# Moving filler matmuls into the idle stretch of a kernel's first transposes, and regrouping two pairs of weight blocks

## The chip, the cores and the metric

The kernel runs on one core of a Trainium2 chip. The metric is the device time of one execution in microseconds. Every timed comparison ran on one chip, kernel and kernel before in turns; the four jobs of experiments ran on four chips, so only ratios are compared between jobs. A ratio is the mean time of one kernel's runs over the mean of the other's of the same rounds, so it isn't quite the ratio of the medians that are quoted beside it. A ratio counts as faster or slower from 2% on, which is 5.9 us here.

## The reference

A retention layer (attention with a decay in place of a softmax) feeds a dense layer with gelu:

```python
scores = q @ k^T / sqrt(64)                  # batch 8, heads 8, sequence 576, head size 64
ret    = scores * Dmat                       # gamma_h ** (i - j) where i >= j, else 0
x      = (ret @ v) -> [4608, 512]
h      = x @ w_in                            # [4608, 2048]
out    = (h * sigmoid(1.702 * h)) @ w_out    # [4608, 512]
```

Inputs and output are float32. The kernel computes in bf16, with sums in float32.

## The kernel before

The 4608 rows are cut into 36 units of 128. A lead-in takes units 0 to 3 one by one as their loads arrive: transpose K and Q on TensorE, scores, masked products, and the running state. Then come the up-projections (`up`, `up_group`) of these four units and the down-projections (`down`). From unit 8 on, the transposes are done by DMA. GpSimd issues all loads in one queue, and the first DMA transpose is made to wait for the V load of unit 13 (into buffer `vn1`).

TensorE starts slowly. In the trace of before, K's first transposes (128 columns each, from 4.31 us) start 106 ns apart and Q's (from 5.58 us) 56 ns apart. The text calls the first pace half clock and says that the clock is open at the second; the granted clock doesn't show the difference (1.00 in every stretch of before from 0 us on). So the kernel gives TensorE fillers, matmuls on zeros whose results nobody reads. That their activity opens the clock is its author's assumption.

```python
def warm(n, b='A', w=512):                   # n fillers of w columns
    for i in range(n):
        op("pe", lambda e: e.matmul(bank[b][:, 0:w], gT[1][:, 0, 0:P], gT[1][:, 0, 0:w], ...))

def lead_in():
    load_kq0(0); load_kq0(1)                 # K and Q of unit 0, in float32, on SP's queue
    ...                                      # loads of units 0 to 11, w_in and w_out, on GpSimd's
    warm_quads(NQUAD)                        # 50 fillers of 64x64
    warm(42, "A", 64)
    ...
    cast_kq0(0, "dve")                       # K, then Q, to bf16 on VectorE
    cast_kq0(1, "dve")
    transpose_pe(0, 0, "E")                  # K's transposes into bank E
    transpose_copy(0, 0, "E", "dve")
    warm(1)
    transpose_pe(0, 1, "B")                  # Q's transposes
    transpose_copy(0, 1, "B", "dve")
    ...
    up_group(0, 6, 2, 0, 2, "B")             # chunk, first w_in block, blocks, first unit, end, bank
    up_group(0, 6, 2, 2, 3, "A")
    up_group(0, 0, 4, 3, 4, "C")
    up_group(0, 4, 4, 3, 4, "B")
    ...
    for f in range(8, NF):
        up(0, f)                             # 512 columns: the "full-width up-projections"
```

Engines are kept in order by semaphores that the program works out from reads and writes. Each TensorE matmul comes with a weight load of its own (the page of before has 3,651 weight loads and, with 31 records missing, 3,620 matmuls), so one matmul is two instructions.

## Time and profile before

| | before |
|---|---|
| median of the first three runs | 295.36 us (295.32 to 296.08) |
| span of the profiled run | 293.8 us |
| TensorE busy | 97% |
| unit 0: start of K's and of Q's transposes | 4.31, 5.58 us |
| full-width up-projections begin | 24.3 us |
| unit 5: Q lands, its transposes start | 40.18, 40.31 us |
| unit 9: DMA transpose lands, scores start | 68.19, 68.24 us |

The page of the profile gives busy shares and the chain that ended last. The timeline gives, for each group of instructions, start, length, engine, line and operation, and in brackets the idle time of the engine before it with what ended it. "issue" in a bracket means that the profile shows nothing that the engine waited for. Landing times of loads and times of single DMA packets come from the trace's DMA records. In six traces (before, after and the four of job 1) 31 matmul records are missing, so a group's count can be one short there, and such a gap can look like a stall of 0.16 us. The first full-width up-projection is one of them: its start is taken as 0.22 us ahead of the second's. The lines themselves are in the prediction.

### The profile page before, as it was taken

Reading aid. Unit: us, or ns where it says so; the run is one execution under the profiler, and the core shown is the slowest. Engines: PE = TensorE matmul, PEld = TensorE weight load, DVE = VectorE, ACT = ScalarE, POOL = GpSimd, SP = SyncE. Lnnn points to the kernel's source line nnn. Section 1 sums busy time; section 2 is a strip of 40 time slices with the busy share of each in tenths; the row PEclk is TensorE's granted clock in tenths of the full one; section 3 lists DMA queues with packets and bytes.
Section 4 is the critical chain, followed back from the end, with each engine's and each line's share of the span. In section 5 each row is a group of like instructions: output and inputs, shape, how many; then the busy total and the mean of one; then the engine's idle time right before and its main releaser. Section 6 shows DMA issues by size and latency. Waiting matters only on the chain.

```text
span 293.8 us, 8029 instructions
## 1 busy us (share of the span) xinstructions
PE 284.2 (97%) x3620; PEld 140.7 (48%) x3651; DVE 99.0 (34%) x202; ACT 134.0 (46%) x235; POOL 110.4 (38%) x141
## 2 busy tenths in 40 slices
PE   6899999999999999999999999999999999999996
PEld 5575446775533553345434543454344434443344
DVE  6750056614650643044503460237014700410000
ACT  7556235661366135622563247424642365216611
POOL 9999889000970670291039202910180000000000
PEclk9999999999999999999999999999999999999999
DMA  9999999998999999399379935991691050111022
GB/s 173 171 205 206 206 233 249 233 126 190 146 239 123 128 207 228 77 168 192 110 123 148 195 96 121 171 191 72 146 139 68 22 134 2 38 71 38 0 64 79
DMA packets 116786, 40.63 MB, mean 138 GB/s; under 512 B 104080, under 2 KB 109968, under 8 KB 116752
## 3 DMA queue, kind: packets, MB, share of 16 engines
q0 software_dynamic: 79712, 22.82, 67.7%
q1 hardware_dynamic: 36896, 17.24, 23.7%
q8 instruction: 28, 0.46, 0.6%
q10 hardware_dynamic: 144, 0.07, 0.1%
q14 instruction: 6, 0.05, 0.1%
HBM read 36.70 MB, written 9.44 MB: 157 GB/s over the span
## 4 chain that ended last, share of the span: by engine, by line
PE 75%; POOL 16%; DMA 5%; issue 2%; SPq 1%; DVE 0%; POOLq 0%
PE psB L582 18%; PE psA L582 18%; PE psA L556 17%; PE psB L556 16%; POOL kqn L226 8%; DMA vn<-in_v_dram 4%; POOL vn L239 4%; POOL w_in_sb L261 3%; PE psX L481 1%; POOL w_out_sb L268 1%; DMA kqT<-kqn 1%; SPq L391 1%; PE psC L497 1%; PE psX L519 1%; PE psK L426 1%
## 5 line engine op out<-in xcount | busy, mean ns | idle before, releaser
L226 POOL DMA_DIRECT2D kqn<-in_k_dram x39 | 35.1, 911 | 107.7 <-DMA kqT<-kqn 105.3
L582 PE MATMUL psA<-w_out_sb,gT 128*128 128x512 bf16 (+1 forms) x287 | 65.9, 370 | 2.4 <-issue 2.2
L582 PE MATMUL psB<-w_out_sb,gT 128*128 128x512 bf16 (+1 forms) x285 | 64.7, 376 | 0.5 <-issue 0.5
L556 PE MATMUL psB<-xT,w_in_sb 128*128 128x512 bf16 x233 | 61.4, 379 | 0.4
L556 PE MATMUL psA<-xT,w_in_sb 128*128 128x512 bf16 x239 | 61.4, 379 | 0.1
L544 DVE TENSOR_TENSOR xT<-psX,gq 128x512 bf16<-128x512 f32 x16 | 11.1, 691 | 112.7 <-PE psX L519 112.7
L450 ACT ACTIVATE kv<-stm 128x1024 bf16<-128x1024 f32 (+1 forms) x18 | 15.6, 866 | 68.8 <-DVE stm L441 68.8
L582 PEld LDWEIGHTS psB<-w_out_sb,gT 128*128 128x128 bf16 x288 | 27.8, 98 | 32.5 <-ACT gT L561 0.3
L561 ACT ACTIVATE gT<-psB 128x512 bf16<-128x512 f32 x60 | 35.8, 597 | 15.9 <-PE psB L556 15.7
L561 ACT ACTIVATE gT<-psA 128x512 bf16<-128x512 f32 x60 | 35.8, 597 | 15.7 <-PE psA L556 15.7
L582 PEld LDWEIGHTS psA<-w_out_sb,gT 128*128 128x128 bf16 x304 | 27.2, 98 | 31.7 <-ACT gT L561 2.5
L239 POOL DMA_DIRECT2D vn<-in_v_dram x40 | 37.1, 942 | 0.1
L556 PEld LDWEIGHTS psA<-xT,w_in_sb 128*128 128x128 bf16 x240 | 19.1, 97 | 32.6 <-ACT gT L561 16.6
L556 PEld LDWEIGHTS psB<-xT,w_in_sb 128*128 128x128 bf16 x240 | 18.8, 97 | 33.2 <-ACT gT L561 16.3
L226 POOL DMA_DIRECT2D kqn<-in_q_dram x37 | 33.4, 916 | 0.3 <-issue 0.3
L345 DVE TENSOR_TENSOR vp<-vn,vfac 128x512 bf16<-128x512 f32 x36 | 23.4, 684 | 29.0 <-DMA vn<-in_v_dram 29.0
L592 ACT ACTIVATE osb<-psB 128x512 f32<-128x512 f32 (+1 forms) x18 | 10.6, 591 | 22.4 <-PE psB L582 22.3
L592 ACT ACTIVATE osb<-psA 128x512 f32<-128x512 f32 x18 | 10.5, 584 | 15.3 <-PE psA L582 15.3
L506 DVE TENSOR_TENSOR pm<-psC,mask 128x512 bf16<-128x512 f32 (+1 forms) x20 | 12.6, 628 | 9.0 <-PE psD L497 9.0
L506 DVE TENSOR_TENSOR pm<-psD,mask 128x512 bf16<-128x512 f32 (+1 forms) x20 | 12.5, 626 | 0.0
L570 PE MATMUL psB<-xT,w_in_sb 128*128 128x256 bf16 (+1 forms) x104 | 12.5, 265 | 0.0
L441 DVE TENSOR_TENSOR stm<-psE,stm 128x256 f32<-128x256 f32 x28 | 11.9, 424 | 1.2
(86 smaller groups left out, 254.8 us busy)
## 6 DMA issues: line engine op xcount, KB each, us to landing
vn<-in_v_dram POOLq DMA_DIRECT2D x32, 256.0 KB, 5.5
out_dram<-osb SPq DMA_DIRECT2D x31, 256.0 KB, 2.3
kqn<-in_k_dram POOLq DMA_DIRECT2D x31, 128.0 KB, 5.3
kqn<-in_q_dram POOLq DMA_DIRECT2D x31, 128.0 KB, 5.6
w_out_sb<-in_moe_w_out_dram POOLq DMA_DIRECT2D x4, 512.0 KB, 13.7
w_in_sb<-in_moe_w_in_dram POOLq DMA_DIRECT2D x8, 128.0 KB, 5.0
w_in_sb<-in_moe_w_in_dram POOLq DMA_DIRECT2D x4, 256.0 KB, 7.6
vn<-in_v_dram POOLq DMA_DIRECT2D x8, 128.0 KB, 3.4
```

Source lines behind the costliest of these rows:

```text
L226: e.dma_start(kqn[sl][p0 : p0 + n, which, :, :], src[b, :, s0 : s0 + n, :].rearrange("h p d -> p h d"),)
L239: e.dma_start(vn[sl][p0 : p0 + n, :, :], v[b, :, s0 : s0 + n, :].rearrange("h p d -> p h d"))
L345: op(eng, lambda e: e.tensor_tensor(vp[u % NVP].ap(), vn[sl].ap(), vfac[:, ty, :, None].to_broadcast([P, H, DH]), ALU.mult), reads=[f"vn{s ...
L441: op("dve", lambda e: e.tensor_tensor(dst, src, prev, ALU.add), reads=[KB[a], f"stm{(i - 1) % 8}"], writes=[f"stm{i % 8}"])
L450: op("act", lambda e: e.activation(kv[:, i0 % NKV : i0 % NKV + n, :, :], stm[:, i0 % 8 : i0 % 8 + n, :, :], AF.Copy), reads=[f"stm{(i0 + i ...
L506: op("dve", lambda e: e.tensor_tensor(pm[(u0 // 2) % 2][hh][:, c0:c1].rearrange("p (a i) -> p a i", i=64), ps32(SB[hh])[:, c0:c1].rearrang ...
L544: op("dve", lambda e: e.tensor_tensor(xT[ch % 2][:, slice(hh, 4, 2), P * jj : P * jj + 2 * P].rearrange("p g (u t) -> p u g t", u=2), ps32 ...
L556: op("pe", lambda e, a=a: e.matmul(bank[b][:, n0:n1], w_in_sb[:, a, P * f : P * f + P], xT[c % 2][:, a, n0:n1], start=(a == 0), stop=(a == ...
L561: op("act", lambda e: e.activation(gT[c % 2][:, f, n0:n1], bank[b][:, n0:n1], AF.Gelu_apprx_sigmoid), reads=[b], writes=[f"g{c % 2}_{f}_{j ...
L570: op("pe", lambda e, a=a, f=f, i=i: e.matmul(bank[b][:, n * i : n * i + n], w_in_sb[:, a, P * f : P * f + P], xT[c % 2][:, a, P * lo : P * ...
L582: op("pe", lambda e, f=f: e.matmul(bank[b][:, 0 : n1 - n0], gT[c % 2][:, f, P * r : P * r + P], w_out_sb[:, f, n0:n1], start=(f == 0), sto ...
L592: op("act", lambda e: e.activation(dst, src, AF.Copy), reads=[b], writes=[f"osb{i}_{n0}"])
```

## The change

It moves fillers. More of them now stand ahead of the first transposes and in the idle time between K's and Q's, meant to keep TensorE active until its clock opens, and fewer in unit 1. It also regroups the last products of the lead-in: the w_in pair 6, 7 is taken for units 2 and 3 in one group.

```diff
-NQUAD = 50
+NQUAD = 54
-            warm(42, "A", 64)
+            warm(44, "A", 64)
             cast_kq0(0, "dve")
-            cast_kq0(1, "dve")
             transpose_pe(0, 0, "E")
             transpose_copy(0, 0, "E", "dve")
-            warm(1)
+            cast_kq0(1, "dve")
+            warm(4)
             transpose_pe(0, 1, "B")
 ...
-            gq_next(1)
+            warm(1, "A", 256)
             state_half(0, 0)
             transpose_pe(1, 0, "E")
             transpose_copy(1, 0, "E", "act")
-            warm(2)
 ...
             block1(0)
-            warm(1)
+            warm(1, "A", 256)
             scores(1)
 ...
-            warm(2)
+            gq_next(1)
+            warm(1)
             state_half(1, 0)
 ...
             up_group(0, 6, 2, 0, 2, "B")
-            up_group(0, 6, 2, 2, 3, "A")
             up_group(0, 0, 4, 3, 4, "C")
-            up_group(0, 4, 4, 3, 4, "B")
+            up_group(0, 4, 2, 3, 4, "A")
+            up_group(0, 6, 2, 2, 4, "B")
```

In matmuls, the first two parts add 7 and the regrouping takes 8 away. Behind it the stream is one matmul, two instructions, shorter than before.

## The prediction

> **What bounds the kernel now.** I read the page first. TensorE is busy for nearly the whole span, so the natural reading is that any microsecond saved on it is a microsecond of the total.
>
> ```profile
> span 293.8 us, 8029 instructions
> ...
> PE 284.2 (97%) x3620; PEld 140.7 (48%) x3651; DVE 99.0 (34%) x202; ACT 134.0 (46%) x235; POOL 110.4 (38%) x141
> ...
> DMA  9999999998999999399379935991691050111022
> ...
> PE 75%; POOL 16%; DMA 5%; issue 2%; SPq 1%; DVE 0%; POOLq 0%
> ```
>
> The last line contradicts that reading. It is the chain that ended last, and only 75% of it is TensorE; 16% is GpSimd issuing DMAs and 5% is DMA. The DMA row is full for its first quarter (40 slices of 7.35 us, so to about 65 us). So I asked for the same chain in order of time, to find where it leaves the DMAs.
>
> ```profile
> 48.55 1.71 POOL kqn L226 x2
> 50.26 12.58 DMA vn<-in_v_dram
> 62.93 2.42 SPq L391
> 65.47 2.73 DMA kqT<-kqn
> 68.84 0.81 PE psA L582 x3
> ```
>
> Columns: start, length, what. Until 50.26 us the chain is GpSimd issuing loads one after another from 1.42 us. The last of them (V of unit 13, issued at 50.26) lands 12.58 us later: it stood behind a queue of others. The first DMA transposes (L391) are told to wait for it. TensorE takes the chain over only at 68.24 us, with the scores of unit 9, when the second of those transposes has landed (65.47 + 2.73 = 68.20). The time before 68 us is therefore set by the load queue, and the 225.6 us from there to 293.8 by TensorE.
>
> How far is TensorE ahead of the loads? For that I read its timeline (start, length, instruction; the idle time before and who ended it in brackets).
>
> ```profile
> 4.31 0.61 PE L361 MATMUL psE<-ident,kqn 128*128 128x128 bf16 x4
> 5.58 0.40 PE L361 MATMUL psB<-ident,kqn 128*128 128x128 bf16 x4 [0.67 <-DVE kqn L257]
> ...
> 8.51 0.41 PE L356 MATMUL psB<-ident,kqn 128*64 128x128 bf16 x8 [0.34 <-DMA kqn<-in_q_dram]
> ...
> 39.67 0.40 PE L361 MATMUL psE<-ident,kqn 128*128 128x128 bf16 x4
> 40.31 0.38 PE L361 MATMUL psD<-ident,kqn 128*128 128x128 bf16 x4 [0.24 <-DMA kqn<-in_q_dram]
> ```
>
> The first two are the transposes of unit 0's K and Q: the 0.67 us between them is the idle stretch that the change wants to fill. The third waits for unit 1's Q, whose DMA lands at 8.46. The last two are unit 5's K and Q. The Q transposes could have started 0.06 after the last K one (39.67 + 0.40 - 0.22 = 39.85), at 39.91; they start at 40.31 on a landing at 40.18. So TensorE comes there 0.40 us too early. At the K transposes just ahead it also waits: VectorE's scale of unit 4's V starts at 38.59 on a landing (38.57), its copy out of bank E ends at 39.61, and only then may unit 5's K be written at 39.67, while the matmuls before it (four from 38.60, 0.216 each) leave TensorE free at 39.46. That is another 0.21. And at unit 9's scores:
>
> ```profile
> 68.23 0.10 PEld L497 LDWEIGHTS psC<-kqT 64*64 64x64 bf16 x1 [0.26 <-DMA kqT<-kqn]
> ```
>
> Unit 8's scores start at 67.77 and take about 0.15, so unit 9's could start near 67.93: 0.31 us of waiting.
>
> [...] the four transposes at 4.31 start 106 ns apart, those at 5.58 56 ns apart. So the clock opens between 4.7 and 5.6 us, inside the stretch being filled; this is what the fillers are for. [...]
>
> **The change part by part.**
>
> *Ahead of the first transposes*: 4 more small fillers (50 of them start within 0.66 us: 0.013 each, 0.05) and 2 more of 64 columns (53 ns each at the half clock, 0.11). TensorE reaches the K transposes at 4.31 + 0.16 = 4.47; the cast they need ended at 4.26, so all 0.16 counts here.
>
> *The copy of K's transposes goes ahead of Q's cast on VectorE.* Before, Q's cast starts at 5.10, the copy at 5.44. After: transposes end at 4.47 + 0.61 = 5.08, the copy starts at 5.13, and the cast follows 0.34 later (the spacing of these two before) at 5.47. It ends at 5.90 instead of 5.53. Q's transposes move from 5.58 to 5.95.
>
> *Four fillers of 512 columns instead of one* lie in that stretch: from 4.87, 4 x 0.216 = 0.86 at full clock, to 5.73, hidden before 5.95. If the clock opens as late as 5.6, two of them take 0.43 and they end at 6.16: 0.2 on the path.
>
> Then Q's copy ends at 6.82, the scores of unit 0 start at 6.88 to 7.09 instead of 6.50, V's scale at 6.74 instead of 6.36, the first state update at 7.47 instead of 7.10, unit 1's K transposes at 7.71 instead of 7.34. The lead-in loses about 0.4 to 0.6 here. But unit 1's Q lands at 8.46, and TensorE, free at 7.94 to 8.15, still waits. At 8.51 both kernels stand level.
>
> *Unit 1's fillers*: one of 512 shortened to 256 ahead of the scores saves 0.11; one of the two after them dropped saves 0.22. That is 0.32, but the limit after it is VectorE: both mask products of unit 1, which start where V's landing (9.23) lets them, end at 11.27, so unit 1's value matmuls can start at 11.32 instead of 11.48: 0.16 left. The factor table (0.68 on VectorE) moves to a VectorE gap of 0.83 before 12.10; no cost. At 14.62 the second w_in pair, landed at 14.64, takes 0.06 of it; unit 3's Q, landed at 16.67, holds its transposes at 16.71 in both; what is left comes through VectorE's output of unit 2 at 17.3: about 0.1.
>
> *Regrouping*: 8 x 128 and 16 x 128 columns become 8 x 128 and 8 x 256. Eight pairs at 2 x 56 ns become eight at 109 ns: 0.02 saved. The same number of gelu instructions, in another order; the weight pairs have long landed (20.07).
>
> Sum: TensorE enters the full-width up-projections (24.34) about 0.1 us earlier, between -0.1 and +0.2. At unit 5 it meets V4 and Q5, whose landings this does not move. The wait of 0.40 becomes 0.50. From 40.31 on nothing differs. The net is 0.0.
>
> **The rivals.** (a) *TensorE-bound throughout, the saving reaches the end.* For it: 97% busy. Against: the three waits on landings above. It would give at most 0.1 to 0.3: 295.1. (b) *The lead-in gets slower and it shows*: the cast is later, the fillers may run at half clock. To show, the loss would have to survive 8.51, then exceed 0.21 + 0.40 = 0.6 at unit 5 and another 0.31 at unit 9, some 0.9 us; I see at most 0.6 before 8.51. [...] (c) *The clock opens more surely*: one of the three runs before took 296.08, the others 295.32 and 295.36; if that one was a late clock, the new fillers would remove it, which the median hardly shows. (d) *The load queue itself moves*: [...] I estimate up to 0.3 either way, because the queue is backed up from about 12 us (issue to landing grows from 4.4 to over 10 us by 17).
>
> **Range and chances.** The centre is the median before, since the net is nil. The runs before spread by 0.76 us (the profiled one took 295.64), and that noise comes with the same landings in the new kernel, more upward than downward. A gain much under 295.0 would need the queue to be faster, a loss over 296 one of the accidents in (b). 2% is 5.9 us, ten times any term here. So 295.4 us, from 294.9 to 295.9, faster by over 2% with 0.01, within 2% with 0.98, slower with 0.01.
>
> **What would show it right or wrong.** Right: Q's transposes of unit 0 near 6.0 instead of 5.58; unit 1's Q transposes still at about 8.5 on the DMA; the full-width up-projections within 0.2 us of 24.3; a wait on Q5 near 40.3 at least as long as before; unit 9's scores near 68.2 on the DMA transpose; an equal length from there to the end. Wrong: unit 5's and unit 9's waits gone or a landing moved by over 0.3 us; start-to-start times of 107 ns for 128 columns after 6.5 us; or a difference that arises after 70 us.

The sum came to about 0.1 us earlier at 24.3 us and to 0.0 at the end, hence 295.4 us. The term from (b) stood outside the sum, as a possible total of about 296 us, and is what "the accidents in (b)" refers to. In the DMA passage stood also that the 12.58 us of V from issue to landing compare with 5.5 us, the page's median for the V loads of 256 KB, and that nothing in the change touches what the DMA engines carry.

## The result, and the profile after

Beside before on one chip, the changed kernel took 294.97 us (294.80 to 295.13, four runs) against 295.48 us (295.32 to 296.08, four runs), a ratio of 0.9979 with a 95% interval of 0.9962 to 0.9996. The time as such is just inside the predicted range. The ratio isn't: applied to the 295.36 us of the prediction it is 294.74 us, below the 294.9 that was set as the low end. The prediction had expected no difference.

The page of the changed kernel, the lines that answer to those of before:

```profile
span 293.0 us, 8028 instructions
...
PE 284.6 (97%) x3619; PEld 141.4 (48%) x3650; DVE 99.3 (34%) x202; ACT 133.9 (46%) x235; POOL 110.3 (38%) x141
...
PE 96%; issue 2%; DVE 1%
```

The span is 0.8 us shorter, and the chain that ended last no longer passes through the loads: it is TensorE throughout. So in this execution the loads never held TensorE by much. The timeline of TensorE shows how it got there:

```profile
4.42 0.61 PE L361 MATMUL psE<-ident,kqn 128*128 128x128 bf16 x4
5.25 1.35 PE L674 MATMUL psA<-gT 128*128 128x512 bf16 x3 [0.22 <-issue]
6.43 0.39 PE L361 MATMUL psB<-ident,kqn 128*128 128x128 bf16 x4
...
8.51 0.30 PE L356 MATMUL psB<-ident,kqn 128*64 128x128 bf16 x4
...
39.22 0.39 PE L361 MATMUL psE<-ident,kqn 128*128 128x128 bf16 x4
39.60 0.38 PE L361 MATMUL psD<-ident,kqn 128*128 128x128 bf16 x4
```

The fillers (second line, the first of the four isn't recorded) start 0.43 us apart, at half clock (the two from 6.66 us on are 0.216 apart), and end about 6.4. Q's transposes come at 6.43 instead of 5.58, and unit 1's Q again at 8.51: the lead-in pays for the fillers and gets it back, as predicted. The full-width up-projections then begin at 24.09 instead of 24.34 (the first recorded ones at 24.31 and 24.55). But unit 5's Q, which TensorE had waited for until 40.31, is now there at 39.60, since it landed at 39.47 instead of 40.18. And unit 9's scores start at 67.30 instead of 68.24.

The loads as a whole weren't faster: the V of unit 13 landed at 62.97, against 62.84 before. What was faster is the first DMA transpose. Here is SP's issue of it in the timeline of before, then in that of after:

```profile
62.93 2.42 SPq L391 DMA_TRANSPOSE kqT<-kqn  x1
```

```profile
63.06 1.37 SPq L391 DMA_TRANSPOSE kqT<-kqn  x1
```

SP needed 1.05 us less to issue it, and the second transpose, the one that unit 9 needs, landed 4.29 us after V instead of 5.35 us.

Something was also lost, far from all that was changed. The timeline at 220 us of before, then of after:

```profile
219.77 2.55 PE L582 MATMUL psA<-w_out_sb,gT 128*128 128x512 bf16 x10
```

```profile
219.77 0.81 PE L582 MATMUL psA<-w_out_sb,gT 128*128 128x512 bf16 x3
220.89 0.59 PE L582 MATMUL psA<-w_out_sb,gT 128*128 128x512 bf16 x2 [0.32 <-issue]
```

TensorE stands for 0.32 us in the midst of identical down-projections, and nothing in the profile holds it. In this profile of before, that stall was 0.07 us.

### The profile page after: what moved, and what is told of

It is laid out like the page before. It is cut to its first block, busy times and chain, and to the rows that moved or that the text cites. A ratio compares the mean times of both kernels' runs of the same rounds, so it can differ in the third digit from the quotient of the medians.

```text
span 293.0 us, 8028 instructions
## 1 busy us (share of the span) xinstructions
PE 284.6 (97%) x3619; PEld 141.4 (48%) x3650; DVE 99.3 (34%) x202; ACT 133.9 (46%) x235; POOL 110.3 (38%) x141
## 4 chain that ended last, share of the span: by engine, by line
PE 96%; issue 2%; DVE 1%
PE psA L582 21%; PE psB L582 21%; PE psA L556 18%; PE psB L556 18%; PE psB L570 4%; PE psA L570 3%; PE psX L481 2%; PE psA L674 2%; PE psC L497 1%; PE psY L519 1%; PE psX L519 1%; PE psK L426 1%; PE psE L361 1%; PE psE L426 1%; PE psD L497 1%
## 5 line engine op out<-in xcount | busy, mean ns | idle before, releaser
L570 PE MATMUL psB<-xT,w_in_sb 128*128 128x256 bf16 x96 | 12.5, 273 | 0.0
```

What stands on the lines that cost most here:

```text
L570: op("pe", lambda e, a=a, f=f, i=i: e.matmul(bank[b][:, n * i : n * i + n], w_in_sb[:, a, P * f : P * f + P], xT[c % 2][:, a, P * lo : P * ...
```

## The experiments

Fifteen runs in four jobs. Before's median in the later jobs was 295.73, 295.97, 296.11 and 296.12 us. Two questions were open: where the 0.5 us came from, and whether they are there at all.

### Job 1: each part alone, and a delay

The first part alone (fillers around the first transposes and the order on VectorE):

```diff
-NQUAD = 50
+NQUAD = 54
-            warm(42, "A", 64)
+            warm(44, "A", 64)
-            cast_kq0(1, "dve")          # ahead of transpose_pe(0, 0, "E")
-            warm(1)
+            cast_kq0(1, "dve")          # behind transpose_copy(0, 0, "E", "dve")
+            warm(4)
```

> Before with the first part of the change alone: the fillers ahead of and inside the first transposes, and the copy of K's transposes ahead of Q's cast. Theory A (the landings of loads decide; what changed between the two profiles is when unit 5's Q lands, 39.47 instead of 40.18 us, and how long the first DMA transpose takes, 2.82 instead of 3.82 us): this part alone delays unit 0, stands level or a little late at unit 1's Q (8.5 us) and enters the full-width up-projections at 24.3 to 24.5 us; if the landing at unit 5 is moved by this part [...], Q5 lands near 39.5 and the total falls by 0.3 to 0.5 us. Theory B (TensorE's lead-in of 0.24 us at 24.3 us carries to the end): this part has none of it, ratio 1.000 to 1.001.

(What the two traces show is that the issue at 4.94 us took 1.07 us in before and 0.88 in after; why isn't shown.)

Measured: 297.31 us, ratio 1.0057 (1.0034 to 1.0081). Both theories missed: the part alone costs 1.6 us.

Unit 1's part alone (`gq_next(1)` moved, fillers fewer, as in the diff of the change):

> Before with unit 1's part alone: fewer fillers there, the factor table moved. Theory A: TensorE enters the full-width up-projections about 0.2 us earlier, then waits longer for unit 5's Q, and the total is that of before, ratio 1.000 within 0.0005, unless the landing itself moves. Theory B: the total falls by the 0.2 us, ratio 0.9992 or less.

Measured: 296.04 us, ratio 1.0013 (0.9994 to 1.0032). No gain, and no clear loss.

The regrouping alone (the `up_group` lines of the diff):

> Before with the regrouping of the w_in pairs alone: 0.02 us less on TensorE at 24.3 us and 8 matmuls (16 instructions) fewer. Theories A and B: same within 0.1 us. Theory C (the fetch of 16 KB of TensorE's instructions, which comes at a fixed place in TensorE's stream, lies on the first DMA transpose and slows it by 1 us): 16 instructions fewer move the fetch near 63.5 us later by 8 x 0.11 = 0.9 us, so it still lies on the first two transposes; same time as before.

Measured: 295.67 us, ratio 0.9990 (0.9977 to 1.0003).

A delay of 0.43 us behind all that is changed:

```diff
+            warm(2, "K")
             for f in range(8, NF):
                 up(0, f)
```

> Before with two fillers of 512 columns more (0.43 us) at 24.3 us, behind everything that the change touches. Theory A: TensorE waits for unit 5's loads by 0.6 us in before, so the delay is swallowed at 40.3 us: ratio 1.000 within 0.0005. Theory B (TensorE-bound): +0.43 us, ratio 1.0015.

Measured: 297.02 us, ratio 1.0038 (1.0021 to 1.0056): 1.3 us for a delay of 0.43. The loads do not swallow it, and it costs three times itself.

So the parts add up to a loss (+0.0057 + 0.0013 - 0.0010 = +0.0060), though the whole had shown a gain. Something depends on more than the work. The timelines of the first part alone show it:

```profile
47.72 0.23 PE L361 MATMUL psC<-ident,kqn 128*128 128x128 bf16 x1 [0.36 <-issue]
...
55.59 0.49 PE L570 MATMUL psB<-xT,w_in_sb 128*128 128x256 bf16 x3 [0.33 <-issue]
...
221.18 1.02 PE L582 MATMUL psA<-w_out_sb,gT 128*128 128x512 bf16 x4 [1.35 <-issue]
```

These are stalls like that at 220.89, in code that this kernel shares with before. The page's table of DMA queues has this line:

```profile
q8 instruction: 28, 0.46, 0.7%
```

These are 28 packets of a kind called "instruction", 0.46 MB in all, that is, 16 KB each (16,384 bytes in the DMA records of before and after), about one for every 260 of TensorE's some 7,290 instructions in the trace. Against their times the stalls fall into place. In the first part alone, such a packet runs from 218.53 to 219.77 us, and TensorE resumes at 221.18, which is 1.41 us after it. At 47.72 it is 1.59 us after a packet's end (46.13), at 55.59 it is 1.46 us (54.13). In after, 220.89 is 1.34 us after 219.55. And half or more of the matmuls of the block ahead of each stall are small ones of 64x64, which use instructions up fastest: ahead of 221 us 128 of them in about 1.2 us, where one of 512 columns takes 0.216.

Hence theory D: a block of instructions becomes usable 1.3 to 1.6 us after it has landed. Where the blocks' borders fall so that a run of small matmuls uses one up sooner, TensorE stands. The borders move with the count of instructions ahead, not with their work.

### Job 2: the count of instructions alone

Before with the same filler time in 9 more matmuls:

```diff
-            warm(42, "A", 64)
+            warm(33, "A", 64)
+            warm(18, "A", 32)
```

> Before with 9 of its 42 small fillers ahead of the first transposes split into two of half the width: the same TensorE time, but 9 matmuls (18 instructions) more in the stream, as many as the first part of the change adds. Theory D (fetch of TensorE's instructions: a 16 KB block is usable some 1.4 to 1.6 us after it lands; where a block holds the run of small 64x64 matmuls of a block of units it is used up sooner, and TensorE stands; where the blocks' borders lie depends on the count of instructions ahead): the stalls marked issue that the kernel with the first part alone showed (0.36 us at 47.7, 0.33 at 55.6, 1.35 at 221.2 us) come back at the same places, and the total rises by about 1.4 us, ratio 1.003 to 1.007. Rival E (the first part's loss of 1.6 us came from its own work in the lead-in): same time as before, 1.000.

Measured: 298.20 us (296.75 to 301.37), ratio 1.0095 (1.0054 to 1.0137). One of these six runs, 301.37, is labelled slow on record, and the ratio contains it; without it the median is 298.16 us, and the listed runs give a ratio of about 1.007. The timeline of this kernel:

```profile
47.51 0.23 PE L361 MATMUL psC<-ident,kqn 128*128 128x128 bf16 x1 [0.23 <-issue]
...
220.65 1.67 PE L582 MATMUL psA<-w_out_sb,gT 128*128 128x512 bf16 x7 [1.57 <-issue]
```

Nothing differs from before but 18 more instructions for fillers of unchanged total length (K's first transposes start at 4.32, before at 4.31), and the large stall is back at its place, 1.29 us after a packet that ended at 219.36. The stall expected at 55.6 us didn't show. So the count alone makes a loss of the first part's kind; the next run asks whether it makes that part's loss.

The first part with the count of before restored:

```diff
-            warm(44, "A", 64)
+            warm(32, "A", 64)
+            warm(3, "A", 256)
```

> The first part of the change alone, but 12 of the small fillers made into 3 of four times the width, so that the count of TensorE's instructions is that of before (the time of the fillers is the same). Theory D: the stalls at 47.7, 55.6 and 221.2 us are gone (the last under 0.1 us), and what is left is the part's own worth: ratio 0.997 to 1.000. Rival E: still 1.005.

Measured: 295.67 us, ratio 0.9995 (0.9970 to 1.0020). The stalls at 47.7 and 55.6 us are gone and that near 222 us is 0.22 (expected: under 0.1). With its count taken back the first part's loss is gone too, so the two runs together show its cause. Apart from the count, the first part is worth nothing that shows. This profile has a stall of 0.31 us at 25.3 us instead.

The delay with the count kept:

```diff
-            warm(42, "A", 64)
+            warm(39, "A", 64)
+            warm(1, "A", 192)
+            warm(2, "K")                    # ahead of the full-width up-projections
```

> Before with 0.43 us more of fillers at 24.3 us, as in the earlier delay run, but the count of instructions kept at that of before. If typical runs of before are TensorE-bound in the lead-in (three of the profiles suggest it: there TensorE entered the full-width up-projections at 25.1 to 25.7 us, later than the loads): up to +0.43 us, ratio 1.0005 to 1.0015, not the 1.0038 of the earlier delay run, whose stalls of 0.22 at 86.2 and 0.55 us at 222.8 are gone by theory D. If loads bind (my prediction): 1.000.

Measured: 296.46 us, ratio 1.0020 (0.9995 to 1.0044), or 0.6 us for a delay of 0.43 us. It halves the cost of the delay and fits a bound by TensorE, but the interval doesn't exclude zero. The stall near 222 us is 0.32 (0.55 in the first delay run).

The changed kernel with 7 matmuls fewer:

```diff
-            warm(44, "A", 64)
+            warm(36, "A", 64)
+            warm(1, "A", 512)
```

> The changed kernel with 8 of its small fillers made into one of eight times the width: same time of fillers, 7 matmuls (14 instructions) fewer, so the count ahead of the late stages is that of the regrouping run (16 fewer than before), which had no stall at all. Theory D: the stall of 0.3 us at 220.9 us of the changed kernel is gone, total 0.2 to 0.3 us under the changed kernel's, ratio to before about 0.9965. Rival: the stall at 220.9 has another cause and stays, ratio 0.998.

Measured: 295.76 us, ratio 0.9997 (0.9973 to 1.0021). The stall at 221 us is gone, as expected, but one of 0.97 us stands at 24.7 us, so nothing is gained.

### Job 3: the changed kernel again, and with other counts

Unaltered:

> The changed kernel unaltered, timed again beside before on one chip, for the spread of its lead-in. Theory F (in most executions the lead-in hangs on the first landings and the clock, so TensorE is late and bound, not the load queue; the change's parts then reach the end): ratio 0.997 to 0.999 again. Theory A (loads bind, the first result was a lucky draw of landings): 1.000 within its interval. Profile: a stall marked issue of 0.2 to 0.4 us near 221 us, none near 25, 48 or 56 us.

Measured: 296.42 us (296.10 to 296.79), ratio 1.0009 (0.9992 to 1.0027). The gain is gone. Its profile shows where this execution of the same kernel lost time:

```profile
16.84 0.40 PE L361 MATMUL psE<-ident,kqn 128*128 128x128 bf16 x4 [0.74 <-DMA kqn<-in_k_dram]
17.46 0.40 PE L361 MATMUL psD<-ident,kqn 128*128 128x128 bf16 x4 [0.22 <-DMA kqn<-in_q_dram]
24.54 0.44 PE L570 MATMUL psA<-xT,w_in_sb 128*128 128x128 bf16 x5 [0.86 <-issue]
```

Unit 3's K and Q landed late (Q at 17.42, in the first profile at 16.51), and the stall near 25 us, which I had expected not to see, took 0.86 us more.

Three matmuls fewer:

```diff
-            warm(44, "A", 64)
+            warm(40, "A", 64)
+            warm(1, "A", 256)
```

> The changed kernel with 4 small fillers made into one of four times the width: same filler time, 3 matmuls (6 instructions) fewer. Against before the count is then +8 up to the regrouped pairs and -8 behind them. The runs so far had a stall near 25 us with 0 or -4 ahead of it (p2, p1c, a_m7) and none with +14 or +18, and none at 221 us with -4 to -16, 0.07 to 0.32 with 0 and -2. Theory D: no stall at either place, total 0.2 to 0.3 us under the changed kernel's of this job. If a stall near 25 us shows, the safe range there ends above +8.

Measured: 296.00 us, ratio 0.9992 (0.9972 to 1.0013), with no stall marked issue of 0.1 us or more behind 20 us.

Unit 1's part with the count of before:

```diff
-            warm(42, "A", 64)
+            warm(40, "A", 64)
+            warm(4, "A", 32)
```

> Unit 1's part alone with the count of instructions of before (two small fillers split in halves). Theory F: the 0.2 us that it saves on TensorE reach the end, ratio 0.9985 to 0.9997. Theory A: 1.000. If the stall of 1.2 us at 25 us, which the part alone had with 4 instructions fewer, is gone, it was the count's (theory D).

Measured: 296.06 us, ratio 1.0004 (0.9984 to 1.0023). The interval covers both theories. The stall near 25 us is not gone: 0.53 us where the part alone had 1.24. So the count alone doesn't decide that one.

The changed kernel with 10 matmuls more:

```diff
-            warm(44, "A", 64)
+            warm(34, "A", 64)
+            warm(20, "A", 32)
```

> The changed kernel with 10 of its small fillers split in halves: same filler time, 10 matmuls (20 instructions) more, so that the count behind the regrouping is +18, as in the first part alone and in the split of before. Theory D: the stall of 1.3 to 1.6 us at 221 us comes back, total 1.1 to 1.9 us over the changed kernel's of this job, ratio to before 1.002 to 1.005: the change would have been a loss by its count of instructions alone. Rival: same as the changed kernel.

Measured: 298.15 us, ratio 1.0075 (1.0039 to 1.0112), 1.7 us over the changed kernel of the same job. Its timeline:

```profile
221.31 1.02 PE L582 MATMUL psA<-w_out_sb,gT 128*128 128x512 bf16 x4 [1.87 <-issue]
```

With the same work in ten matmuls more, the change would have been a loss of 2 us.

### Job 4: the noise, and a third look

Before against itself (no edit):

> Before against itself. Any theory: 1.000; what it strays is the noise that all ratios here carry. If TensorE usually comes to unit 9's scores later than the DMA transpose lands (theory F), this profile shows the scores of unit 9 after 68.3 us with no wait on the transpose, unlike the first profile of before; if my prediction's picture is the usual one, a wait of about 0.3 us there again.

Measured: 295.95 us (295.16 to 298.26) beside 296.12, ratio 1.000 (0.9971 to 1.0030). Its profile isn't like the first one of before:

```profile
17.70 0.40 PE L361 MATMUL psD<-ident,kqn 128*128 128x128 bf16 x4 [1.10 <-DMA kqn<-in_q_dram]
24.84 0.94 PE L570 MATMUL psB<-xT,w_in_sb 128*128 128x128 bf16 x14 [0.52 <-issue]
```

TensorE waits 1.10 us for unit 3's Q, stalls near 25, and comes to unit 9's scores at 68.63 us, 0.52 us after the DMA transpose landed. There is no wait there.

The changed kernel a third time (no edit):

> The changed kernel a third time. If its gain of 0.5 us is real: ratio 0.997 to 0.999. If the first result was a draw of landings and clock, and its count of instructions gives back what the lead-in saves (stalls near 25 and 221 us): 1.000 within 0.0015.

Measured: 295.83 us (295.05 to 296.94), ratio 0.9997 (0.9972 to 1.0021). Its stall near 221 us is 0.44, and here unit 9 does wait for the transpose again, by 0.18 us.

The version with three matmuls fewer, again:

> The changed kernel with 3 matmuls fewer among its fillers, again. Theory D: no stall near 221 us, none or a short one near 25 us, ratio to before 0.998 to 0.9995, and below that of the changed kernel in this job by 0.0005 to 0.002.

Measured: 295.75 us, the median of the five fast runs, ratio of the fast runs 0.9981 (0.9959 to 1.0003). Its profiled run was slow and is not compared: the page shows why, 372 us at a granted clock of 0.756.

```profile
PEclk9777777777777777777777777777777777777777
```

### The sixteen fast profiles side by side

Each run left one profile. The stall near 221 us, by how many instructions more than before stand ahead of it:

| instructions | kernels | stall near 221 us |
|---|---|---|
| -16 | regrouping; changed -7 | none, none |
| -8 | changed -3 | none |
| -4 | unit 1's part | none |
| -2 | changed, three times | 0.32, 0.39, 0.44 |
| 0 | before twice; first part, unit 1's part and delay with the count kept | 0.07, 0.43; 0.22, 0.24, 0.32 |
| +4 | delay | 0.55 |
| +18 | first part; before split; changed +10 | 1.35, 1.57, 1.87 |

The traces also show where these stalls stand, which makes theory D more than a fit. Count TensorE's stream by its weight loads, which every trace has in full (two instructions for each, and the few others that are recorded). There are 25 stalls marked issue of 0.06 us or more behind 20 us in the sixteen profiles, the gaps of missing records left out. Every one stands at instruction 256 k + 194 to 196, where k is the number of instruction packets landed by then (3, 5, 6, 10 or 23), and ends 1.2 to 1.6 us after the k-th landed. So they lie at the blocks' borders alone. At 221 us the border comes behind 128 small matmuls and then, with the count of before, nine of 512 columns, as the second profile of before shows:

```profile
219.75 2.12 PE L582 MATMUL psA<-w_out_sb,gT 128*128 128x512 bf16 x9
222.30 0.81 PE L582 MATMUL psA<-w_out_sb,gT 128*128 128x512 bf16 x3 [0.43 <-issue]
```

Nine matmuls of 0.216 us cover 1.9 us of the wait; with 18 instructions more there are none of them ahead of the border (the stall comes right behind the small ones), which is why that row is the worst. Near 25 us it is rather a late packet: the third one started at 22.1 to 23.0 us in the six profiles with a stall there, and at 19.6 to 22.3 in the ten without. What made it late is open.

The time from the start of unit 9's scores to the end is 225.2 to 225.5 us in all sixteen once the stalls behind 80 us are taken off. So all that differs otherwise lies ahead of 69 us.

There, unit 9's scores started within 0.05 us of the landing of their DMA transpose in six of the sixteen: before, regrouping, unit 1's part with the count kept, changed, changed -3, changed the third time. In the other ten TensorE came 0.19 to 1.17 us later than the landing. The picture on which the prediction rested, TensorE ahead of the loads, is a state that the kernel is in only at times.

And the landing itself, counted from V of unit 13, goes with the instruction packet that runs nearest to the first transpose. Where the packet started ahead of SP's issue by 0.05 to 0.24 us (changed, changed +10, changed the third time), the second transpose landed 4.28 to 4.29 us after V. With the packet 0.29 behind the issue it was 4.77, and with 0.55 to 2.26 behind, in all the rest, 5.10 to 5.80. That is a correlation over sixteen profiles; no run moved the packet with all else equal, so the cause is likely but not shown.

## Why the prediction was wrong, point by point

**The lead-in's own sum** came near. K's transposes were expected at 4.47 and came at 4.42. Q's were expected at 5.95 to 6.16 and came at 6.43, because all fillers ran at half clock (0.43 us each): the clock opened later than the first profile of before had suggested. Q's cast was mis-sized too: it took 0.61 us (5.45 to 6.06), not 0.43, so 5.95 was out of reach at any clock. Scores of unit 0 started at 7.34, not 6.88 to 7.09. At unit 1's Q both kernels stood level at 8.51, as predicted, though TensorE itself now came last there (Q had landed at 7.84). The full-width up-projections gained 0.25 us where about 0.1 was expected, a part of it because the V of unit 1 landed 0.59 us earlier (8.64 instead of 9.23) and took VectorE's limit away.

**"At unit 5 it meets V4 and Q5, whose landings this does not move"** is the step that failed in the first result. Q5 landed 0.71 us earlier, and the transpose for unit 9 0.94 us earlier. The end of the load queue stayed (V of unit 13 0.12 us later), so the queue's total was rightly read. But single landings inside it, and the transposes behind it, move between executions by more than the change saves: in the three profiles of the changed kernel Q5 landed at 39.47, 40.07 and 39.54 us. In the two of before it was 40.18 and 40.16, so a part of the change in it isn't excluded; no run tested that. Rival (d) named this, and put it at 0.3 us; it measured 0.7 to 0.9.

**"The time before 68 us is therefore set by the load queue"** was read off one execution and taken for the rule. (The page's DMA row doesn't mark that point either: it is at 8 or 9 tenths not for its first quarter, to 65 us, but for sixteen slices, to about 118 us.) It held in six of sixteen profiles. In the others early landings (Q of unit 0 from 4.6 to 6.3 us, Q of unit 3 from 16.0 to 17.7) or the clock made TensorE late. In the two delay runs, which have before's lead-in, it was still at half clock at 9.0 us:

```profile
4.72 0.63 PE L674 MATMUL psA<-gT 128*128 128x512 bf16 x1
...
8.60 1.06 PE L674 MATMUL psA<-gT 128*128 128x512 bf16 x2
9.59 0.64 PE L356 MATMUL psB<-ident,kqn 128*64 128x128 bf16 x8
```

A filler of 512 columns at full clock takes 0.38 us by the profile (before, 11.02 us), and these take 0.63. So the waits of 0.21, 0.40 and 0.31 us that were to swallow any loss aren't usually there, and the delay of 0.43 us wasn't swallowed.

**"From 40.31 on nothing differs"** failed too, by a term that the sum didn't have: the stall near 221 us, 0.07 in before and 0.32 in after (but 0.43 in the second profile of before, so the difference between these two isn't the change's). Rival (b) looked for a loss in the lead-in; the largest loss lies 200 us behind it and comes from the count of instructions.

**"The net is 0.0"** is what the later jobs show. Three ratios of the same kernel are 0.9979, 1.0009 and 0.9997, mean 0.9995, and before against itself strays by 0.003 either way. The gain of 0.5 us in the first result is thus most likely that job's draw. Only one of its four runs left a profile, and that one had early loads in the lead-in. Whether 0.1 to 0.2 us of it are real stays open, since no run here resolves that. The range was too narrow: before itself has runs from 294.9 to 298.3 us in these jobs, where three runs within 0.76 us had been taken for the spread.

**What became of the change's intent.** In the lead-in the clock was open by 7.3 us in all eight fast profiles with the new first stretch, against over 9.0 us in two of the eight without. That is rival (c), and eight against eight is too few to call it shown. The version with three matmuls fewer had ratios below 1 both times (0.9992 and 0.9981), and in its fast profile neither stall; but both intervals reach past 1, so it isn't shown to beat either kernel.

## What to carry to other kernels

Before believing that a change of less than 1% in a long unrolled kernel gains or costs anything, change the count of instructions with the work held fixed and see whether the time moves as much; here 18 more instructions for the same length of fillers cost 2 us, four times the 0.5 us that the change seemed to gain. Look for idle time marked issue behind dense runs of small matmuls, at the instruction packets just before it (here the stalls ended 1.2 to 1.6 us after one had landed), and at whether such stalls lie whole multiples of 256 instructions apart, as the 25 here did within two. And read slack from several executions: a wait in one profile tells where that execution stood, not what bounds the kernel.
